# Sinkhorn by matmul, re-paced loads and crossbar transposes, and o a unit later, in a fused attention and FFN kernel on one core

## Chip, cores and metric

One core of a Trainium2 chip. The time is device microseconds of that core; spans (first to last instruction of a profiled execution) are about 1.8 us shorter than times. A transfer is *issued* when an engine puts it into its queue and *lands* when its data has arrived; "landed after" counts from the issue. With one core a run is called slow when it is over 1.5% above the fastest run of the same kernel in its session, otherwise fast. Ratios are the mean of one kernel's fast runs over the mean of the other's fast runs of the same rounds on the same chip, so they are not quite the ratios of the medians that are quoted beside them.

## The reference

```python
P = sort_net                                   # (4, 8, 8, 8)
for _ in range(5):                             # Sinkhorn
    P = exp(P - max(P, -1))
    P = P / (sum(P, -1) + 1e-9)
    P = P / (sum(P, -2) + 1e-9)
k_sorted = einsum('bhij,bhjcd->bhicd', P, k_blocks)      # 8 blocks of 96 rows, head dim 64
v_sorted = einsum('bhij,bhjcd->bhicd', P, v_blocks)
attn = softmax(q_blocks @ k_sorted.T / 8)                # inside each block
x = (attn @ v_sorted), heads side by side                # 3072 x 512
out = ((x @ w_a) * (x @ w_b)) @ w_out                    # d_ff 1536
```

q, k, v are 4 x 8 x 768 x 64, all in float32.

## The kernel before, cut

The work is done in 16 pairs of heads, g = 0 to 15, four to a batch (HP = 4). A pair goes through four steps. *mix*: k and v are mixed by P. *scores*: q times k and the exponential. *o*: times v, and normalized into xp. *xT*: xp transposed into the FFN's operand. Batch 0 is done in two halves with transposes on the matrix engine (PE). Batches 1 to 3 use crossbar transposes, DMA_TRANSPOSE, issued by SyncE (SP): q into qTf, mixed v into vs, xp into xT. GpSimd (POOL) issues all loads, which convert to bf16. The attention of batch b+1 is cut into "units" that are threaded between the FFN steps of batch b.

```python
for it in range(5):                       # Sinkhorn: 32 partitions (one a head), 64 elements each
    nc.scalar.activation(out=p_nat, in_=p_nat, func=AF.Exp)
    nc.vector.reduce_sum(out=rsum, in_=p_nat, axis=AX.X)
    nc.vector.reciprocal(out=rsum, in_=rsum)
    nc.vector.tensor_mul(...)             # rows
    nc.vector.reduce_sum(out=csum, in_=p_nat.transpose([0, 2, 1]), axis=AX.X)
    nc.vector.reciprocal(out=csum, in_=csum)
    nc.vector.tensor_mul(...)             # columns; then replicate, transpose by matmul, spread
...
def c_(g):                                # mix
    if g == HP:
        stage_q(g)                        # q transpose by crossbar, SP
    if g + 1 < B * HP:
        stage_q(g + 1)
    if g + 2 < B * HP:
        pair_q(g + 2)                     # GpSimd copy of q, ahead of its transpose
    if g + HP < B * HP:
        load_pair((g + HP) // HP, g % HP) # k, v, q of the pair one batch on
    stage_mix(g, "k", ("act",))
    stage_mix(g, "v", ("dve", "act"))     # ends with the v transpose by crossbar
def o_(g):
    stage_o(g)
    to_xT(g)                              # xp transpose by crossbar
for n in range(HP + 1):
    if n < HP: us.append(c_(g0 + n))
    if n > 0:  us.append(o_(g0 + n - 1))
    if n < HP: us.append(stage_scores(g0 + n))
```

`us.append(x(...))` stands for a closure. FFN steps are `ffn_ab` (eight matmuls of 384 columns, 1.3 us) and `ffn_out`, a "po step" (twelve of 512 columns, 2.6 us). The units are spread evenly over the number of steps, so that all are done two steps before a batch's end at the latest.

The softmax here doesn't subtract the row's maximum and nothing guards it: scores larger than these inputs give would overflow.

## Time and profile before

| | |
|---|---|
| median of the first 3 runs | 256.21 us (253.7 to 257.01) |
| profiled span | 252.7 us |
| PE busy | 234.4 us, 93% |
| PE waits for vs (v's crossbar transpose) | 5.4 us in two waits |

First, from the page of the kernel before, the span in 40 slices of 6.3 us. Digits are tenths; PEclk is the granted PE clock, and DMA the mean busy share of the 16 DMA engines.

```profile
PE   0999899969958999999999999999999999999993
PEclk9999999999997999999999999999999999999999
DMA  6999999999999998992332343332244210000122
```

PE is full but for its start, slice 9 and slices 12 and 13 (counted from 1), where it waits; in slice 13 the clock falls once. The DMA queue is full until about 115 us. The view of waits of PE names the two dips (us in total, times, the longest):

```profile
PE o_ps L241 <- DMA vs<-vT: 5.4, 2, 3.3
```

In PE's timeline (start, duration, line, tile, count) the later of them, and the end of batch 0, look so:

```profile
76.44 1.04 PE L241 MATMUL o_ps<-vs,eT 96*128 96x65 bf16 x16 [3.33 <-DMA vs<-vT]
77.29 4.02 PE L351 MATMUL po<-w_out_sb,hT 128*128 128x512 bf16 x12
...
84.29 0.66 PE L241 MATMUL o_ps<-vs,eT 96*128 96x65 bf16 x16
84.79 7.93 PE L351 MATMUL po<-w_out_sb,hT 128*128 128x512 bf16 x35
92.56 0.97 PE L323 MATMUL pf<-xT,w_a_sb 128*128 128x384 bf16 x4
```

After 3.33 us of waiting the sixteen o matmuls take 1.04 instead of 0.66 us and twelve po matmuls 4.02 instead of 2.76 (x11 and x35 stand for 12 and 36: some matmul records are missing from a trace): the wait is paid again in slow clock. Then o of the last pair at 84.29 us, three po steps, and batch 1's first FFN matmuls, which need its xT. SP's timeline of the same time:

```profile
69.06 5.00 SPq L262 DMA_TRANSPOSE qTf<-qc  x1
74.16 4.56 SPq L283 DMA_TRANSPOSE vs<-vT  x1
...
86.53 1.30 SPq L309 DMA_TRANSPOSE xT<-xp  x1
88.36 6.29 SPq L358 DMA_DIRECT2D out_dram<-o_sb  x6
94.75 1.27 SPq L262 DMA_TRANSPOSE qTf<-qc  x1
```

The view of the tile xT, narrowed to the transpose issued at 86.53 us, has its landing:

```profile
L309 SPq DMA_TRANSPOSE xT<-xp x1: 1301/1301/1301, 86.5 to 86.5; - x1
...
DMA to landing us min/median/max: 6.6/6.6/6.6
```

So the last xT landed at 93.1 us. PE's first three matmuls of batch 1 need pairs 0 to 2 only; the fourth needs the last pair.

At the start, two of the exponentials in ScalarE's timeline give a Sinkhorn round, 1.76 us; PE's timeline gives the first mix, a 512-column filler (a matmul whose result nobody uses, there to keep PE busy), and the first FFN matmul:

```profile
4.12 0.26 ACT L374 ACTIVATE p_nat<-p_nat 32x64 f32<-32x64 f32 x1 [1.50 <-DVE p_nat L387]
5.88 0.26 ACT L374 ACTIVATE p_nat<-p_nat 32x64 f32<-32x64 f32 x1 [1.50 <-DVE p_nat L387]
```

```profile
12.20 0.38 PE L191 MATMUL mixh<-s_all,k 128*64 128x64 bf16 x12
...
14.12 0.39 PE L166 MATMUL mixh<-warm 128*128 128x512 bf16 x1
...
20.59 0.66 PE L323 MATMUL pf<-xT,w_a_sb 128*128 128x384 bf16 x3
```

### The profile page before, as it was taken

To read this page: it belongs to the slowest core of one execution; us is meant where nothing else is said; L and a number is where in the kernel's file an instruction comes from. 1 tells how busy PE (TensorE), PEld (TensorE's weight loads), DVE (VectorE), ACT (ScalarE), POOL (GpSimd) and SP (SyncE) were. 2 spreads that over 40 slices of the span, in tenths; PEclk is the share of its full clock that TensorE was granted. 3 is DMA by queue.
4 is the path that set the end of the run, shared out by engine and by line. 5 is a ranking of instruction groups with operands and counts; after the bars stand their busy time and mean duration, and the time that the engine had idled before them with its cause. 6 is when DMAs were issued, how large, how long until landed. Compare 5 with 4: busy or idle time off the path is not lost.

```text
span 252.7 us, 5448 instructions
## 1 busy us (share of the span) xinstructions
PE 234.4 (93%) x2219; PEld 135.6 (54%) x2229; DVE 108.2 (43%) x259; ACT 102.4 (41%) x202; POOL 61.4 (24%) x83
## 2 busy tenths in 40 slices
PE   0999899969958999999999999999999999999993
PEld 0475566536624455666654456666654466665441
DVE  6775456535613313555453133645533144444111
ACT  3385555556520217463740137465440033333010
POOL 8974678554715305300100000000000000000000
PEclk9999999999997999999999999999999999999999
DMA  6999999999999998992332343332244210000122
GB/s 88 197 199 196 197 200 201 190 169 184 146 129 199 239 204 160 160 116 45 72 65 83 115 118 73 67 74 40 42 35 125 113 44 0 0 0 4 52 114 83
DMA packets 56441, 28.67 MB, mean 113 GB/s; under 512 B 33376, under 2 KB 53344, under 8 KB 56416
## 3 DMA queue, kind: packets, MB, share of 16 engines
q0 software_dynamic: 20944, 14.16, 40.6%
q1 hardware_dynamic: 35472, 14.17, 28.9%
q8 instruction: 17, 0.28, 0.4%
q14 instruction: 8, 0.07, 0.1%
HBM read 28.32 MB, written 6.29 MB: 137 GB/s over the span
## 4 chain that ended last, share of the span: by engine, by line
PE 83%; DMA 9%; DVE 5%; ACT 1%; issue 1%; DVEq 0%
PE pf L323 46%; PE po L351 24%; DMA vs<-vT 8%; PE o_ps L241 3%; PE mix L272 3%; PE sc L293 2%; PE mixh L191 2%; PE vs_ps L218 1%; PE sc L206 1%; PE xt_ps L232 1%; DMA p_nat<-in_sort_net_dram 1%; DVE hT L344 1%; DVE xph L247 1%; DVE csum L384 1%; ACT p_nat L374 1%
## 5 line engine op out<-in xcount | busy, mean ns | idle before, releaser
L344 DVE TENSOR_TENSOR hT<-a_sb,pf 128x384 bf16<-128x384 bf16 x95 | 52.6, 554 | 74.0 <-PE pf L323 45.5
L323 PE MATMUL pf<-xT,w_a_sb 128*128 128x384 bf16 x380 | 78.1, 327 | 0.0
L323 PE MATMUL pf<-xT,w_b_sb 128*128 128x384 bf16 x380 | 77.5, 326 | 0.0
L343 ACT CAST a_sb<-pf 128x384 bf16<-128x384 f32 x95 | 45.5, 479 | 65.9 <-PE pf L323 49.4
L351 PE MATMUL po<-w_out_sb,hT 128*128 128x512 bf16 x279 | 64.5, 385 | 0.5
L323 PEld LDWEIGHTS <-w_b_sb 128*128 128x128 bf16 x384 | 37.5, 98 | 25.1 <-issue 0.6
L323 PEld LDWEIGHTS <-w_a_sb 128*128 128x128 bf16 x384 | 34.6, 98 | 22.1
L351 PEld LDWEIGHTS <-hT 128*128 128x128 bf16 x288 | 28.0, 99 | 33.3 <-issue 1.6
L162 DVE COPY o_sb<-po 128x512 f32<-128x512 f32 x12 | 8.3, 692 | 47.8 <-PE po L351 31.3
L160 ACT COPY o_sb<-po 128x512 f32<-128x512 f32 x12 | 7.0, 586 | 43.0 <-PE po L351 23.1
L298 ACT ACTIVATE eT<-sc 96x768 bf16<-96x768 f32 x24 | 18.1, 802 | 12.4 <-PE sc L293 12.4
L256 POOL COPY qc<-q 128x768 bf16<-128x768 bf16 x12 | 9.9, 826 | 53.1 <-DMA qTf<-qc 34.0
L241 PE MATMUL o_ps<-vs,eT 96*128 96x65 bf16 x256 | 11.6, 196 | 6.1 <-DMA vs<-vT 5.4
L247 DVE TENSOR_TENSOR xp<-o_ps,rec 96x512 bf16<-96x512 f32 x24 | 15.5, 680 | 0.3
L241 PEld LDWEIGHTS <-eT 96*128 96x128 bf16 x256 | 10.5, 99 | 8.9 <-issue 6.3
L160 ACT CAST kT<-mix 128x384 bf16<-128x384 f32 x24 | 10.3, 482 | 6.2 <-PE mix L272 6.2
L94 POOL DMA_DIRECT2D v<-in_v_dram x16 | 11.5, 718 | 1.8 <-DMA w_b_sb<-in_moe_w_b_dram 0.8
L94 POOL DMA_DIRECT2D k<-in_k_dram x16 | 11.5, 719 | 1.2 <-DMA w_a_sb<-in_moe_w_a_dram 0.6
L245 DVE RECIPROCAL rec<-o_ps 96x8 f32<-96x8 f32 x32 | 5.2, 185 | 12.1 <-PE o_ps L241 12.0
L94 POOL DMA_DIRECT2D q<-in_q_dram x12 | 8.6, 719 | 1.3 <-DMA w_a_sb<-in_moe_w_a_dram 0.7
L175 PE MATMUL q_ps<-ident,q_first 64*64 64x64 bf16 x96 | 3.0, 217 | 6.2 <-DMA q_first<-in_q_dram 6.2
L210 ACT ACTIVATE eT<-sc 96x768 bf16<-96x768 f32 x8 | 6.5, 808 | 2.5 <-PE sc L206 2.5
(69 smaller groups left out, 138.4 us busy)
## 6 DMA issues: line engine op xcount, KB each, us to landing
out_dram<-o_sb SPq DMA_DIRECT2D x18, 256.0 KB, 2.0
k<-in_k_dram POOLq DMA_DIRECT2D x16, 192.0 KB, 6.4
v<-in_v_dram POOLq DMA_DIRECT2D x16, 192.0 KB, 6.8
q<-in_q_dram POOLq DMA_DIRECT2D x12, 192.0 KB, 9.1
w_a_sb<-in_moe_w_a_dram POOLq DMA_DIRECT2D x6, 256.0 KB, 10.8
w_b_sb<-in_moe_w_b_dram POOLq DMA_DIRECT2D x6, 256.0 KB, 10.7
w_out_sb<-in_moe_w_out_dram POOLq DMA_DIRECT2D x3, 512.0 KB, 10.9
out_dram<-o_sb SPq DMA_DIRECT2D x12, 128.0 KB, 5.1
```

The lines of the kernel that those rows point to most:

```text
L94: nc.gpsimd.dma_start(out=to, in_=_ap(t, base, [[W, P], [S * D, 2], [1, W]]))
L160: nc.scalar.copy(out=out, in_=in_)
L162: nc.vector.tensor_copy(out=out, in_=in_)
L241: nc.tensor.matmul(o_ps[:, e, i * (D + 1):(i + 1) * (D + 1)], lhsT=eT[:, hf, e, i * BLK:i * BLK + P], rhs=vs[0:BLK, i0 + i, V0 - 1 + e * ( ...
L247: nc.vector.tensor_tensor(out=_ap(xp, i0 * 2 * D, [[nxp * 2 * D, BLK], [D, 2], [2 * D, NBH], [1, D]]), in0=_ap(o_ps, 1, [[1024, BLK], [511 ...
L256: nc.gpsimd.tensor_copy(out=qc.rearrange("p c e d -> p e c d"), in_=loaded[g][2].rearrange("p e (c d) -> p e c d", c=NCH))
L272: nc.tensor.matmul(mix[e * D:(e + 1) * D, c // 3, c % 3 * P:(c % 3 + 1) * P], lhsT=src2[:, e, c * D:(c + 1) * D], rhs=s_all[:, 2 * g + e], ...
L298: nc.scalar.activation(out=eT[:, hf, :, 0:HB], in_=sc[0:BLK, :, 0:HB], func=AF.Exp, scale=float(scale))
L323: nc.tensor.matmul(pf[:, 0:HW], lhsT=w_sb[:, kc, m * P:(m + 1) * P], rhs=x_cols(b, kc, t), start=(kc == 0), stop=(kc == KA - 1))
L343: nc.scalar.copy(out=a_sb, in_=pf[:, 0:HW])
L344: nc.vector.tensor_mul(out=hT[:, m, t * HW:(t + 1) * HW], in0=a_sb, in1=ab[1][:, 0:HW])
L351: nc.tensor.matmul(po, lhsT=hT[:, m, c * P:(c + 1) * P], rhs=w_out_sb[:, m, :], start=(m == 0), stop=(m == KO - 1))
```

## The change

Its intent: a shorter Sinkhorn, by spreading it over 128 partitions, and no waits for vs, by keeping loads away from the transposes and giving v's transpose more time. Cut to its core:

```diff
 # Sinkhorn: partition = (head, column), 16 heads at a time, 8 elements each
+def sink_sum(g, it, ps):            # row sums by an fp32 matmul with a 128x128 block matrix
+    lhs, rhs = (sk[g, "rows"], is_block) if it == 0 else (heads, sk[g, "e"])
+    nc.tensor.matmul(ps, lhsT=lhs..., rhs=rhs, start=True, stop=True)
+def sink_vec(g, it, ps):            # reciprocal, multiply, reduce, reciprocal
+    ...
-    keep_busy(heat[:, 0], 8)        # filler matmuls before the first mix
+    # 2 fillers in rounds 1 and 2, 1 before the first mix
 # heads 0-15 at the start; heads 16-31 as six "turns" in FFN steps of batch 0's second stage,
 # the last of which lets GpSimd spread their P
 ...
 # q of batch 1: all its loads first, then all four copies and transposes
-for hp in range(2): load_pair(1, hp)
+for hp in range(HP): load_pair(1, hp)
 ...
-pair_q(HP); pair_q(HP + 1); for hp in range(2, HP): load_pair(1, hp)
+for g in range(HP, 2 * HP): pair_q(g); stage_q(g)
 def c_(g):
-    stage_q(g), stage_q(g + 1), pair_q(g + 2), load_pair(next batch)
     stage_mix(g, "k", ...); stage_mix(g, "v", ...)
 def o_(g):
     stage_o(g)
     to_xT(g)
+    if 2 * HP <= g + 2 < B * HP:
+        pair_q(g + 2); stage_q(g + 2)
+    if g + HP < B * HP:
+        nc.gpsimd.tensor_copy(out=gate, in_=st[g, "xp"][...one element])   # the "gate"
+        load_pair((g + HP) // HP, g % HP)
 # order of units: c_(g), scores(g), o_(g-1) instead of c_(g), o_(g-1), scores(g)
 # spacing: a po step counts as two ab steps (paced), two po steps left at the end
```

The spacing has a consequence: batch 0 now has two po steps after its last o instead of three, and batches 1 and 2 have three instead of four. Small things left out of the cut: the order of two loads at the start, the order of two units of batch 0's second half, and four buffers instead of three for q.

## The prediction

> **What bounds it now.** The matrix engine. The page has PE busy 234.4 of 252.7 us; the chain of waits that ended last is 83% PE. From 90 to 240 us the table of stretches shows PE busy in full; gains can come only from before:
>
> 1. Start: PE's timeline has the first mix at 12.20 us. Until then the chain is Sinkhorn on 32 partitions: each round is one exponential and six VectorE operations of 0.19 to 0.27 us, 1.76 us a round, then p_fin, p_rep, pc_ps, s_all, 1.29 us.
> 2. Two waits of the o matmuls for the crossbar transpose of v (vs): 2.12 us at 57 us and 3.33 us at 76 us (waits of PE, 5.4 us). After the second the clock fell: o takes 1.04 instead of 0.50 us and twelve po matmuls 3.83 instead of about 2.6. Together about 7.4 us. Alone a transpose lands in 3.0 us, beside the loads of batch 2 in 8 to 13, and SyncE's queue is in order: the v transpose of 74.16 us stood behind a q transpose that took 5.0 us to issue.
>
> **What changes.**
> - Sinkhorn, half of the heads: a round becomes an exponential, one small fp32 matmul and four VectorE operations on 8 elements a partition. The Trainium skill, "FP8 and Floating Point Precision", section TensorE Precision Notes, gives true fp32 four passes; no run here shows it yet. From pc_ps (four bf16 pairs, 0.36 us from operand ready to reader started) I estimate 0.45 us for the matmul. With 0.75 for VectorE and 0.30 for the exponential a round is about 1.5 us: 0.25 saved, four times. The tail loses a step (0.4 us). Against it: masks and memsets before round one, and a load in 32-byte pieces, 0.4 us. Net 0.8 us earlier.
> - The other half moves into batch 0's second stage: five fp32 matmuls and one more, about 1.8 us of PE, in PE's program order, each behind a VectorE and ACT round trip of about 2 us where a step gives 1.3 to 2.1. Estimate: 1.8 us of work, 1 us of stalls.
> - Loads of batch 2 wait for xp, q transposes of batch 1 go early, and o comes a unit later: v's transpose gets about 9 us instead of 4 to 5, on quieter queues. Both waits go, and the clock drop with them: 7.4 us less about 0.5.
> - New danger: batch 0's last o now leaves two po steps (5.2 us) instead of three before batch 1 needs its xT, and the late loads fall beside that transpose (6.6 us in this trace at 80 to 87 us). I charge 0.8 us at about 90 us.
>
> Sum: -0.8 -6.9 +2.8 +0.8 = -4.1 us for the profiled run. The profiled run took 254.5; the median, 256.2, probably holds larger transpose waits, which go too: about -6.
>
> **Predicted: 250.2 us**, range 247.3 to 253.3; faster by over 2% 0.63, within 2% 0.35, slower 0.02.
>
> **Right if:** waits of PE for vs below 1 us; no clock slice under 0.9 after the start; first mix at 11 to 11.8 us; rounds of 1.4 to 1.6 us; chain_b matmuls of group 1 with PE waits for ACT around 45 to 58 us; 90 to 240 us unchanged in length.
>
> **Wrong if:** the fp32 matmul takes well over 0.5 us (no gain at the start, more stall in stage 2); PE waits for xT near 88 us by 2 us or more, with a clock drop; the loads, now later, miss their mixes; or the turns hide entirely and the run lands below 248.

## The result, and the profile after

The result was correct and slower: 270.87 us median of four runs (270.58 to 279.17), against 256.61 us for before with one more run; the ratio of fast runs is 1.059, 95% interval 1.048 to 1.071. It is outside the predicted range and on the other side of before.

The same views after. The slices:

```profile
PE   3699899999999809999899958999999999999993
PEclk9999999999999977999999997999999999999999
DMA  6999999981599993018888895113141620000132
```

The waits of PE; vs is gone from the list, xT is at its top:

```profile
PE pf L382 <- DMA xT<-xp: 12.0, 2, 7.7
...
PE sc L352 <- DMA qTf<-qc: 0.9, 1, 0.9
```

The end of batch 0 in PE's timeline, then SP's and GpSimd's around it:

```profile
86.81 0.66 PE L300 MATMUL o_ps<-vs,eT 96*128 96x65 bf16 x16
87.52 5.12 PE L410 MATMUL po<-w_out_sb,hT 128*128 128x512 bf16 x23
92.49 0.65 PE L382 MATMUL pf<-xT,w_a_sb 128*128 128x384 bf16 x3
100.84 0.48 PE L382 MATMUL pf<-xT,w_a_sb 128*128 128x384 bf16 x1 [7.71 <-DMA xT<-xp]
```

```profile
85.96 1.21 SPq L368 DMA_TRANSPOSE xT<-xp  x1
87.27 1.24 SPq L321 DMA_TRANSPOSE qTf<-qc  x1
88.61 2.54 SPq L417 DMA_DIRECT2D out_dram<-o_sb  x2
91.24 1.53 SPq L368 DMA_TRANSPOSE xT<-xp  x1
92.86 3.19 SPq L321 DMA_TRANSPOSE qTf<-qc  x1
```

```profile
86.58 0.72 POOL L109 DMA_DIRECT2D k<-in_k_dram  x1 [0.34 <-issue]
...
90.38 0.72 POOL L109 DMA_DIRECT2D k<-in_k_dram  x1
```

The view of the tile xT, for the transpose issued at 91.24 us:

```profile
L368 SPq DMA_TRANSPOSE xT<-xp x1: 1527/1527/1527, 91.2 to 91.2; - x1
...
DMA to landing us min/median/max: 9.6/9.6/9.6
```

The last o starts at 86.81 us; its transpose is issued 4.4 us later (2.2 before), behind a q transpose and two stores in SP's queue; it lands 9.6 us after that (6.6 before), beside the loads that the gate released at 86.58 and 90.38 us; and one po step of cover is missing. That is 2.2 + 3.0 + about 2.6 us, the wait of 7.71 us. Afterwards nine FFN matmuls and a mix of k and v run on a slow clock, 1.8 us more. The end of batch 1 repeats it with a wait of 4.26 us.

The start, in ScalarE's and PE's timelines:

```profile
6.78 0.30 ACT L189 ACTIVATE e<-rc,c 128x8 f32<-128x8 f32 x1 [1.58 <-PE heat L180]
8.74 0.30 ACT L189 ACTIVATE e<-rc,c 128x8 f32<-128x8 f32 x1 [1.66 <-DVE c L216]
```

```profile
7.14 0.59 PE L205 MATMUL chain_a<-e,heads 128*128 128x8 f32 x2 [0.42 <-ACT e L189]
...
14.19 0.53 PE L250 MATMUL mixh<-s_all,k 128*64 128x64 bf16 x12 [0.47 <-DVE vs L151]
...
16.73 0.61 PE L180 MATMUL mixh<-warm 128*128 128x512 bf16 x1
...
25.46 0.67 PE L382 MATMUL pf<-xT,w_a_sb 128*128 128x384 bf16 x3
```

A round is 1.96 us, longer than before. The first mix comes 2.0 us later and the first FFN matmul 4.9 us later: the other 2.9 us lie in the attention between them, most of which runs on a slow clock; the same filler takes 0.61 instead of 0.39 us.

Where the 16.4 us of span went, by starts read from PE's timelines (us per stage; the last stage is to the end of the span). The other three columns are runs described below; the last is of a slow run, so it is not compared in time.

| stage | before | after | old start | gate only | gate, order, q (slow run) |
|---|---|---|---|---|---|
| to the first FFN matmul | 20.6 | 25.5 | 21.1 | 21.3 | 21.6 |
| to the first mix of batch 1 | 26.8 | 27.5 | 27.5 | 26.8 | 26.8 |
| to the first po step | 23.0 | 21.6 | 25.5 | 24.4 | 28.2 |
| to batch 1's first FFN matmul | 22.2 | 18.0 | 18.0 | 17.1 | 17.1 |
| to batch 2's | 54.7 | 65.1 | 65.0 | 55.0 | 69.2 |
| to batch 3's | 54.5 | 60.5 | 60.4 | 54.5 | 54.5 |
| to the end | 51.0 | 51.0 | 50.9 | 51.0 | 51.0 |

The forecast gain is there, 5.6 us in the third and fourth rows. It is lost twice over: 5.6 us in the first two rows, and 16.4 us in the rows of batches 1 and 2, which begin at the ends of batches 0 and 1: 12.0 us of waits for xT, one wait of 0.9 us for qTf, and nearly all the rest slow clock after the waits.

### The profile page after: what moved, and what is told of

The parts are those of the page before. It is cut to its first block, busy times and chain, and to the rows that moved or that the text cites. A ratio compares the mean times of both kernels' runs of the same rounds, so it can differ in the third digit from the quotient of the medians.

```text
span 269.1 us, 5501 instructions
## 1 busy us (share of the span) xinstructions
PE 241.0 (90%) x2226; PEld 141.2 (52%) x2238; DVE 111.3 (41%) x277; ACT 104.0 (39%) x207; POOL 62.1 (23%) x90
## 4 chain that ended last, share of the span: by engine, by line
PE 79%; DMA 10%; DVE 5%; ACT 2%; issue 1%; SPq 1%; DVEq 0%; ACTq 0%
PE pf L382 43%; PE po L410 20%; DMA xT<-xp 7%; PE mix L331 4%; PE o_ps L300 3%; DMA qTf<-qc 2%; PE sc L352 2%; PE mixh L250 2%; PE chain_a L205 1%; DVE hT L403 1%; PE vs_ps L277 1%; PE sc L265 1%; DMA p_nat<-in_sort_net_dram 1%; PE xt_ps L291 1%; SPq L417 1%
## 5 line engine op out<-in xcount | busy, mean ns | idle before, releaser
L382 PE MATMUL pf<-xT,w_a_sb 128*128 128x384 bf16 x380 | 79.1, 329 | 12.0 <-DMA xT<-xp 12.0
L382 PE MATMUL pf<-xT,w_b_sb 128*128 128x384 bf16 x380 | 78.7, 330 | 0.0
L410 PE MATMUL po<-w_out_sb,hT 128*128 128x512 bf16 x277 | 63.2, 379 | 0.7 <-issue 0.2
L410 PEld LDWEIGHTS <-hT 128*128 128x128 bf16 x288 | 27.3, 98 | 31.4
L357 ACT ACTIVATE eT<-sc 96x768 bf16<-96x768 f32 x24 | 18.2, 803 | 6.7 <-PE sc L352 6.7
L552 POOL COPY gate<-xp 1x1 bf16<-1x1 bf16 x8 | 1.4, 180 | 54.4 <-DVE xp L306 54.4
L315 POOL COPY qc<-q 128x768 bf16<-128x768 bf16 x12 | 9.9, 836 | 11.7 <-DMA q<-in_q_dram 11.7
L300 PEld LDWEIGHTS <-eT 96*128 96x128 bf16 x256 | 10.6, 99 | 3.2 <-ACT eT L269 0.7
L300 PE MATMUL o_ps<-vs,eT 96*128 96x65 bf16 x256 | 11.6, 196 | 0.6 <-ACT eT L269 0.6
L166 POOL TENSOR_TENSOR s_all<-mask,p_col 128x1024 bf16<-128x1024 bf16 (+1 forms) x4 | 6.7, 1696 | 20.2 <-DVE p_col L587 20.1
L176 DVE CAST vT<-mix 128x384 bf16<-128x384 f32 x12 | 6.7, 558 | 4.5 <-PE mix L331 4.5
```

The source lines that it names most:

```text
L176: nc.vector.tensor_copy(out=out, in_=in_)
L300: nc.tensor.matmul(o_ps[:, e, i * (D + 1):(i + 1) * (D + 1)], lhsT=eT[:, hf, e, i * BLK:i * BLK + P], rhs=vs[0:BLK, i0 + i, V0 - 1 + e * ( ...
L315: nc.gpsimd.tensor_copy(out=qc.rearrange("p c e d -> p e c d"), in_=loaded[g][2].rearrange("p e (c d) -> p e c d", c=NCH))
L357: nc.scalar.activation(out=eT[:, hf, :, 0:HB], in_=sc[0:BLK, :, 0:HB], func=AF.Exp, scale=float(scale))
L382: nc.tensor.matmul(pf[:, 0:HW], lhsT=w_sb[:, kc, m * P:(m + 1) * P], rhs=x_cols(b, kc, t), start=(kc == 0), stop=(kc == KA - 1))
L410: nc.tensor.matmul(po, lhsT=hT[:, m, c * P:(c + 1) * P], rhs=w_out_sb[:, m, :], start=(m == 0), stop=(m == KO - 1))
```

## The experiments

Eighteen more kernels were run; all gave correct results. "Before" medians varied from 255.6 to 258.0 us from session to session, so ratios are given. Medians are over all runs, slow ones too; ratios are of fast runs alone; spans are of the profiled run.

| run | this, median us | ratio to before (95%) | span | PE waits in the profile, us |
|---|---|---|---|---|
| after | 270.9 | 1.059 (1.048 to 1.071) | 269.1 | xT 12.0, qTf 0.9 |
| old_start | 270.9 | 1.052 (1.042 to 1.062) | 268.4 | xT 11.7, qTf 5.4 |
| old_pace | 259.1 | 1.006 (0.999 to 1.013) | 257.0 | xT 1.7, vs 0.6 |
| no_gate | 266.4 | 1.035 (1.028 to 1.042) | 264.4 | xT 7.6 |
| spare4 | 267.5 | 1.038 (1.029 to 1.047) | 265.0 | qTf 4.2, xT 1.7, o_sb 1.9 |
| pe_last_x | 265.0 | 1.039 (1.035 to 1.043) | 262.5 | qTf 6.7, o_sb 1.7 |
| delay | 261.8 | 1.028 (1.023 to 1.032) | 260.0 | vs 5.9 |
| o_later | 256.1 | 0.996 (0.989 to 1.003) | 251.5 | vs 3.1 |
| gate_only | 251.0 | 0.984 (0.977 to 0.991) | 250.0 | vs 1.9, xT 0.3 |
| gate_paced | 254.7 | 0.994 (0.985 to 1.003) | 253.2 | xT 5.0, vs 0.5 |
| gate_o_later | 252.4 | 0.987 (0.979 to 0.994) | 251.1 | xT 2.8 |
| gate_newq | 254.8 | 0.994 (0.984 to 1.005) | 254.1 | qTf 4.8, xT 1.0 |
| gate_newsink | 254.3 | 0.985 (0.974 to 0.996) | 252.8 | xT 0.8 |
| gate_paced_o | 259.4 | 1.004 (0.984 to 1.024) | 259.4, slow run | xT 8.5 |
| gate_paced_q | 261.3 | 1.010 (0.986 to 1.035) | 258.7 | qTf 5.0, xT 3.3 |
| gate_o_q | 269.1 | none, one fast run | 268.3, slow run | qTf 9.4, xT 6.0 |
| fix_pe | 253.4 | 0.990 (0.979 to 1.002) | 248.7 | vs 0.9, o_sb 0.8 |
| after_oldq | 265.0 | 1.036 (1.024 to 1.047) | 263.5 | vs 3.1, xT 2.4 |
| warm_sink | 255.3 | none, one fast run | 249.3 | xT 0.4 |

### The two halves apart

**old_start** is the changed kernel with before's Sinkhorn.

```diff
-    sink_exp / sink_sum / sink_vec / turns, heads 0-15 at the start
+    the Sinkhorn loop of before, all heads, keep_busy(heat[:, 0], 8)
```

> The changed kernel with the Sinkhorn of before (32 partitions, all heads at the start, its eight filler matmuls), everything else of the change kept. Theory A, two separate causes: the new Sinkhorn costs the 4.9 us by which the first pf matmul came later (25.5 against 20.6 us) and about 2 us in its turns, the new pacing costs the rest by waits for xT at the ends of batches 0 and 1. Then: first pf at 20.5 to 21 us, PE waits for xT still 8 us or more in sum, time 262 to 266 us. Rival B: the xT waits come from the Sinkhorn too, because its second half held GpSimd, and so the loads behind it, until 70.6 us. Then: xT waits below 2 us in sum and time 248 to 252 us.

Measured: first FFN matmul at 21.1 us, just above A's range, xT waits of 11.7 us, as A said, but 270.9 us: nearly as slow as the whole change. B is out: with no second half of Sinkhorn the xT waits stay. A's sum is out too, because the 4.4 us won at the start were lost again in the third row of the table, at a new wait in PE's timeline:

```profile
55.05 0.52 PE L294 MATMUL sc<-qTf,kT 64*128 64x96 bf16 x16 [4.23 <-DMA qTf<-qc]
```

The q transposes of batch 1 now wait for all its loads. They were issued from 43.4 us on and landed at 55 us, whatever PE does; a later start hides this, an earlier one shows it.

**old_pace** is before with the new Sinkhorn alone.

```diff
-    the Sinkhorn loop of before
+    sink_exp / sink_sum / sink_vec, heads 16-31 in turns; loads, q, units, spacing of before
```

> The kernel of before with the new Sinkhorn alone (both halves of it, the second in turns), and the loads, q transposes and units of before. Theory A: first pf at 25 to 26 us, PE waits for vs of 3 to 7 us as before, PE waits for xT below 1 us, time 261 to 265 us. Rival B: the xT waits of 8 us or more are there too and the time is 266 us or more.

Measured: first FFN matmul at 26.3 us, but only 0.6% slower, the wait for vs nearly gone (0.6 us), and a wait for xT of 1.7 us, a little above A's and far below B's. So the new pacing is what costs, and B is wrong here too. Why the later start cost so little was a new question. GpSimd's timeline suggests an answer: its spread of the second half's P stood in its queue until the turns were done, and the loads of batch 2's last two pairs (issued at 73.58 and 76.54 us) stood behind it.

```profile
69.09 3.77 POOL L166 TENSOR_TENSOR s_all<-mask,p_col 128x1024 bf16<-128x1024 bf16 x2 [10.19 <-DVE p_col L580]
```

That would be a gate by accident. It is a reading, not shown, and gate_newsink below speaks against it as the whole answer. A rival reading, that until 76 us the DMA queue sets the time and so any late start is absorbed, was tested with **delay**:

```diff
-            keep_busy(heat[:, 0], 8)
+            keep_busy(heat[:, 0], 28)
```

> The kernel of before with 28 instead of 8 filler matmuls ahead of the first mix: PE starts its real work about 4.5 us later, nothing else is changed. Theory C: until about 76 us the time is set by the DMA queue (loads and the transposes beside them), so a later start is taken out of the waits for vs. Then first pf at 25 us, waits for vs fall from 5.4 to below 2 us, and the time rises by less than 2 us, to 256 to 258.5 us. Rival D: PE's start is on the critical path, as the prediction had it. Then the time rises by the whole delay, to 260.5 to 261.5 us.

Measured: first FFN matmul at 26.05 us, waits for vs still 5.9 us, and 2.8% slower, about 7 us. Theory C is wrong; loads are issued from inside the units, so they move with PE. D is right in kind; the loss is even larger than the delay of 5.5 us, the rest being slow clock after the waits (0.76 to 0.90 of full in three stretches of 5 us).

### Inside the changed kernel

**no_gate** and **spare4** each undo one thing.

```diff
-                nc.gpsimd.tensor_copy(out=gate, in_=st[g, "xp"][0:1, NB - 1, 1, D - 1:D])
```

> The changed kernel without the one-element GpSimd copy that makes each load of the next batch wait for xp; GpSimd then issues the loads as soon as it reaches them. Theory A1: the last xT transpose of a batch is late because the gate puts the last loads beside it. Then its landing falls from 9.6 to 4 to 6 us, the PE waits for xT fall from 12.0 to 4 us or less, some wait for vs may come back, and the time is 259 to 264 us. Rival A2: the last o simply comes too near the batch's end, and SyncE's queue holds it up; then landing or issue stay late, the waits stay above 8 us and the time is 268 us or more.

Measured: 266.4 us, between the two theories. The xT waits fell to 7.6 us, but the last two xT transposes still landed 9.2 and 9.6 us after issue: without the gate GpSimd went on issuing loads, a pair every 2 to 7 us, from 72 to 111 us, across the end of the batch. The gate alone is not the cause.

```diff
-        paced(ab, po, units_full(b + 1) if b + 1 < B else [], 2)
+        paced(ab, po, units_full(b + 1) if b + 1 < B else [], 4)
```

> The changed kernel with all units done four po steps before the end of a batch instead of two; the gate stays, so the loads move forward with the last o. Rival A2 (too little cover): xT waits fall from 12.0 to below 3 us with landing still 8 to 10 us, time 258 to 262 us. Theory A1 (the loads beside it) alone: the transposes still land late, 8 to 10 us after issue, and the cover of about 10 us hides most of it, so A1 also predicts a fall here; what tells them apart is the landing time in the run without the gate. If neither is right the waits stay above 8 us.

Measured: xT waits 1.7 us with landings of 10.6 and 10.7 us, as A2 said, but 267.5 us instead of 258 to 262. The wait moved: scores of batch 2 waited 4.2 us for qTf, and an FFN matmul 1.9 us for the copy of an output tile (o_sb).

**pe_last_x** takes the last xp of a batch off the crossbar: eight PE transposes and two copies, in a unit of its own.

```diff
             stage_o(g)
-            to_xT(g)
+            if g % HP < HP - 1:
+                to_xT(g)
+        us.append(lambda: x_(g0 + HP - 1))      # PE transposes of the last pair
```

> The changed kernel, but the last pair of each batch brings its xp to xT by eight PE transposes and two copies, as the first batch does, instead of by the crossbar; all loads, the gate and the other transposes stay. If the late crossbar transpose of the last xp is what costs at the ends of batches 0 and 1, the PE waits for xT fall from 12.0 us to below 1.5, the clock stays at 1.0 around 100 and 160 us, and the time falls from 270.9 to 255 to 260 us. If the ends of the batches wait for something else (q or v transposes of the next batch, or the loads themselves), a wait of 5 us or more turns up at another tile near 100 us and the time stays above 264 us.

Measured: no wait for xT at all, and yet 265.0 us. Scores waited 6.7 us for qTf instead, in three places. So neither "the xT wait" nor "the cover" is the cause by itself; take one late transpose out of the way and the next one shows.

### From before upwards

Two single pieces on before. **o_later** is only the order of units:

```diff
-                if n > 0:
-                    us.append(lambda g=g0 + n - 1: o_(g))
                 if n < HP:
                     us.append(lambda g=g0 + n: stage_scores(g))
+                if n > 0:
+                    us.append(lambda g=g0 + n - 1: o_(g))
```

> The kernel of before with only the order of units changed: scores before the o of the pair before (o a unit later). v's transpose gets one unit more, 2 to 3.5 us, so the waits for vs fall from 5.4 to below 2 us. Against it, scores come a unit earlier and their q transposes do not: by the trace of before the q transpose of pair 7 landed at 81.2 us and its scores started at 81.25 us, so a wait of scores for qTf of 2 to 4 us should appear. If that trade is right the time stays within 2 us of before; if the q transposes move forward too, it falls to 249 to 252 us.

Measured: same time, waits for vs 3.1 us, and the foreseen wait for qTf did not come. **gate_only** is only the loads:

```diff
 def c_(g):
-    if g + HP < B * HP:
-        load_pair((g + HP) // HP, g % HP)
 def o_(g):
     stage_o(g)
     to_xT(g)
+    if g + HP < B * HP:
+        nc.gpsimd.tensor_copy(out=gate, in_=st[g, "xp"][0:1, NB - 1, 1, D - 1:D])
+        load_pair((g + HP) // HP, g % HP)
```

> The kernel of before with only the loads moved: each load of the next batch is issued after the o of its pair and waits for xp, as in the change. If the gate is what puts loads beside the last xT transpose, PE waits for xT appear at the ends of batches 0 and 1 (before leaves three po steps of cover, not two, so 1 to 5 us in sum) while the waits for vs fall below 1.5 us; time 252 to 258 us. If the gate is innocent, no xT wait appears and the time is 248 to 251 us.

Measured: 0.984 of before, an interval clear of 1, though not clear of 2%. The wait for xT is 0.3 us. **The gate is the good part of the change**; with before's three po steps of cover it does no harm. It is faster than both kernels. One wait for vs is left, and PE's timeline shows what even a short one costs:

```profile
57.65 0.65 PE L242 MATMUL o_ps<-vs,eT 96*128 96x65 bf16 x16 [1.95 <-DMA vs<-vT]
58.14 1.04 PE L324 MATMUL pf<-xT,w_a_sb 128*128 128x384 bf16 x4
58.97 1.49 PE L324 MATMUL pf<-xT,w_b_sb 128*128 128x384 bf16 x4
```

Eight FFN matmuls take 2.25 us from start to next start (58.14 to 60.39), where before has 1.40 at the same place; the following scores and four more matmuls lose another 0.7.

### One part more

Each of the next four adds one part of the change to gate_only: the spacing (the `paced` loop), the order of units, the late q transposes (`pair_q`, `stage_q` moved as in the change), and the new Sinkhorn. Their edits are the parts of the diff above.

> The run with only the gate (251.0 us) plus only the new spacing of units, which counts a po step as two ab steps and leaves two po steps after the last o of batch 0 instead of three (three instead of four for batches 1 and 2). Theory E1, too little cover under the gate: PE waits for xT rise from 0.3 us to 4 us or more, with a clock drop, and the time is 255 to 262 us. If the spacing is innocent, xT waits stay below 1 us and the time is 249 to 252.5 us.

Measured: the xT wait of 5.0 us came with its slow clock; 254.7 us, at the edge of the expectation, same as before.

> The run with only the gate plus only the order of units (scores before the o of the pair before). The one wait for vs left with the gate, 1.9 us, should go, and no wait for xT come, as the last unit of a batch is the last o either way: 247.5 to 250.5 us. If the gate, which follows o, now brings the loads later and nearer the batch's end, an xT wait of 1 us or more appears and the time is 251 to 254 us.

Measured: the wait for vs went, and an xT wait of 2.8 us came: the last two o are now neighbours, so the loads behind the last but one fall beside the last xT transpose, which lands after 9.4 us instead of 6.9. No gain, no loss.

> The run with only the gate plus only the new q transposes: those of batch 1 all together after all its loads, those of later batches after the o of two pairs before instead of one stage before their scores. Theory E2: scores wait for qTf of batch 1 near 50 us by about 4 us, because the transposes start only when the last load of batch 1 and the w_out loads are issued, and the q transposes beside the last xT cost up to 2 us more of xT wait; time 254 to 260 us. If the q transposes are innocent, no wait for qTf over 1 us and 249 to 252 us.

Measured: scores wait 4.8 us for qTf at 55 us and FFN matmuls 1.0 us for xT, as E2 said; the slowest of these spans.

> The run with only the gate plus the new Sinkhorn. In the run with the new Sinkhorn alone, its second half held GpSimd until 69.1 us and so delayed the loads of batch 2, a gate by accident; with the gate in both, that gain is no longer in the difference. Theory F: the new Sinkhorn costs what it costs at the start (first pf 4.9 to 5.7 us later) and in its turns (1.5 to 3 us), together 6 to 8 us: 257 to 259.5 us. Rival: it is nearly free, as its 0.6% alone said: below 253.5 us.

Measured: ratio 0.985, as gate_only's. Theory F is wrong in size: the first FFN matmul came at 25.15 us, 3.8 us later than in gate_only, but the span only 2.8 us later. The later start again let the loads land, and the 1.95 us wait for vs was gone. With the gate in both kernels the new Sinkhorn is still nearly free, so the accidental gate can't be the main reason why it was so in old_pace.

So three parts of the pacing each cost 0.3 to 1% on top of the gate, by ratios from two chips whose intervals overlap. Added, their single spans give 250.0 + 3.2 + 1.1 + 4.1 = 258.4 us; together (old_start, with the small things named above) they gave 268.4. About ten microseconds belong to the combination, more than the spread of one kernel's fast runs (2 to 4 us), and pairs were run to find it.

> Gate, spacing and order together, old q transposes. Theory G (shared slack): each part takes a bite of one reserve, the time from the last o of a batch to the first need of its xT; a part alone is nearly free, parts together cost in full. Then the wait for xT at the end of batch 0 is 6 us or more (5.0 and 2.8 alone, 0.3 with the gate alone) and a wait of 1 to 4 us appears at the end of batch 1, where no part alone had one: 257 to 262 us. Rival H (the parts add, and the q transposes are the rest): the spans add to 250.0 + 3.2 + 1.1, so 255 to 256.5 us, no wait at the end of batch 1.

Measured: xT waits 8.5 us, among them the foreseen new one at the end of batch 1, 2.23 us; 256 to 261 us. The times alone do not decide between G and H. The profiled run is slow, and its start fell on a slow clock (first FFN matmul at 24.9 us), so its xT waits, which look like G's, settle nothing.

> Gate, spacing and new q transposes, old order of units. Theory G: the wait for qTf near 52 us stays at 4 to 5 us, the wait for xT at the end of batch 0 is 5 to 8 us, a wait of up to 2 us at the end of batch 1; 260 to 264 us. Rival H: the spans add to 250.0 + 3.2 + 4.1, so 258 to 260 us.

Measured: 256.7 to 263.8 us; the profiled run is fast, 260.5 us, where the ranges of G and H meet; its span of 258.7 us is 1.4 above H's sum; the xT wait, 3.3 us, is smaller than G said.

> Gate, order and new q transposes, old spacing. Theory G: the wait for qTf near 52 us stays at 4 to 5 us, the wait for xT at the end of batch 0 is 3 to 6 us, none at the end of batch 1 (four po steps of cover); 257 to 260 us. Rival H: 250.0 + 1.1 + 4.1, so 256 to 258 us; or, if the last missing 10 us sit in order and q together, 262 us or more.

Measured: 263.2 us in the only fast run and 269 to 270 in the others, against 253 to 260 for before in the same rounds. The last branch of H was hit, by one fast run: the missing time sits in order and q together. The view of waits of PE (of a slow run, so its sizes are not to be relied on; the fast run too is 6 us above the additive 257):

```profile
PE sc L294 <- DMA qTf<-qc: 9.4, 3, 4.6
...
PE pf L324 <- DMA xT<-xp: 6.0, 1, 6.0
```

In the old arrangement a q transpose goes into SP's queue one pair ahead of its scores, before the mix. In the new, it goes in behind the o of two pairs before; with o a unit later and scores a unit earlier, only one mix is left between. And at a batch's end the order puts xT, q, xT, q closely after each other into SP's queue, with the loads that the gate releases: in old_start, a fast run, at 85.54, 86.85, 89.47 and 92.15 us. There the last xT landed 10.7 us after its issue, 13.8 us after its o started (11.6 and 14.8 us in the slow run of gate_o_q).

The three pairs can also be read as old_start less one part (on another chip, and without the small things named above). With all three parts the ratio is 1.052; without the late q transposes (gate_paced_o) 1.004, without the order (gate_paced_q) 1.010, with intervals clear of old_start's. Without the spacing (gate_o_q) the one fast run stays over 3% above before's fast runs of its session. So most of old_start's loss needs order and late q transposes both.

### Back in the changed kernel

**after_oldq** puts only the q transposes of the changed kernel back.

```diff
 def c_(g):
+    if g == HP: stage_q(g)
+    if g + 1 < B * HP: stage_q(g + 1)
+    if g + 2 < B * HP: pair_q(g + 2)
 def o_(g):
-    if 2 * HP <= g + 2 < B * HP: pair_q(g + 2); stage_q(g + 2)
 # and batch 1's loads and q transposes in two pairs, as in before
```

> The changed kernel with only its q transposes put back (batch 1's in two pairs of loads, every later one at the mix of the pair before its scores). Theory I: in the whole change the late q transposes together with the later o are the main cost, as in the pair of the two alone. Then the waits for qTf are below 1 us, the wait for xT at the end of batch 0 falls from 7.7 to 3 to 6 us and the time from 270.9 to 258 to 263 us. Rival: cover and gate are enough for the loss; then xT waits stay above 10 us in sum and the time is above 266 us.

Measured: no wait for qTf, xT waits 2.4 instead of 12.0 us, and 265.0 us, 5.9 us better by medians but 2 us short of the expectation (ratio 1.036 instead of 1.059). The xT wait fell by more than the time because another transpose was late:

```profile
90.47 1.04 PE L300 MATMUL o_ps<-vs,eT 96*128 96x65 bf16 x16 [3.12 <-DMA vs<-vT]
```

So late q transposes account for some two fifths of the loss here, and not for all of it. Nor do they stand out: undoing the gate (1.035), giving more cover (1.038) or taking the last xT off the crossbar (1.039) takes back as much within the noise, and each time a wait for some late transpose or output copy was left. No single part is the cause. Undoing only the order, or only the spacing, in the full change was not tried.

### The start

**warm_sink** is gate_newsink with 21 fillers instead of 5 during the Sinkhorn (the expectation says 22; what it calls passes are the two records of each fp32 matmul in the trace).

```diff
+    keep_busy(heat[:, 0], 5)
     for it in range(5):
-        if it == 1 or it == 2: keep_busy(heat[:, 0], 2)
+        keep_busy(heat[:, 0], (2, 3, 4, 2, 3)[it])
-    keep_busy(heat[:, 0], 1)
+    keep_busy(heat[:, 0], 2)
```

> Gate and new Sinkhorn (254.3 us, span 252.8), with 22 filler matmuls of 512 columns instead of 5 during the Sinkhorn, so that PE is at full clock in it. Theory J: the new Sinkhorn's rounds are long because its fp32 matmul runs on a slow clock (0.59 us for its two passes at the start, 0.39 us in the second stage), and the attention of batch 0 after it too. Then rounds fall from 1.96 to 1.70 to 1.80 us, the first mix comes at 12.9 to 13.4 us, the first pf at 21 to 22 us instead of 25.15, and the time falls by 2 to 4 us, to 250.5 to 252.5. If the fillers stand in the matmul's way, rounds stay at 1.9 us or more and the first pf above 24 us.

Measured: half right. The first FFN matmul came at 21.9 us instead of 25.15, and the profiled span was 249.3 instead of 252.8 us. But rounds stayed at 1.86 to 1.95 us, the first mix came at 13.58 us, and of the four times one was 251.1 and three 255.2 to 255.7, so the gain in time is not shown. The fp32 matmul does shrink at full clock:

```profile
8.96 0.36 PE L205 MATMUL chain_a<-e,heads 128*128 128x8 f32 x2
```

The rounds did not follow: the first three sums still took 0.59 to 0.60 us, the clock being up only from about 9 us on, and in the fourth round a copy of q on ScalarE stood before the last exponential. But from the first mix to the first FFN matmul it took 8.36 us, as in before (8.39), where gate_newsink took 11.27: with the fillers that stretch is at full clock again. pe_last_x gives more evidence, by chance. It has the start of the changed kernel to the letter, and there the clock came up early (PE's timeline):

```profile
16.54 0.39 PE L180 MATMUL mixh<-warm 128*128 128x512 bf16 x1
...
23.01 0.66 PE L382 MATMUL pf<-xT,w_a_sb 128*128 128x384 bf16 x3
```

Filler 0.39 instead of 0.61 us; first mix at 14.00 against 14.19 us, first FFN matmul at 23.01 against 25.46. So of the 4.9 us 2.0 lie before the first mix and 2.3 are slow clock after it; the last 0.6 us was not followed up.

### A version faster than both

**fix_pe** joins the gate, the order, and the last xT by PE, with everything else of before.

> Gate and order of the change, with the q transposes, spacing and Sinkhorn of before, and the last pair of each batch brought to xT by PE transposes. No PE wait for vs or xT over 0.5 us should be left between 45 and 200 us, for about 1 us of PE transposes: 247.5 to 250.5 us, faster than before by 2 to 3%. If waits move to qTf or to the copies, it stays at 251 us or above, the time with the gate alone.

Measured: 250.5 to 254.8 us; by fast runs 0.990 of before, interval 0.979 to 1.002. Its profiled span, 248.7 us, is the shortest of all, with no wait over 0.8 us after 50 us, but its time is not shown to be below before's. Three versions have an interval wholly below 1: gate_only (0.984), gate_newsink (0.985) and gate_o_later (0.987); they all have the gate, and gate_only is the simplest.

## Why the prediction was wrong

- **"Both waits go": right.** The vs waits fell from 5.4 us to none, their slow clock with them: 5.6 us won in the third and fourth stages, against 4.1 forecast for them (6.9 less 2.8 for the turns, which lie there too).
- **"New danger ... I charge 0.8 us at about 90 us": this is the step that failed.** The mechanism was named, its size was off twentyfold: 16.4 us in the two stages after batch ends (12.0 of it waits for xT), not 0.8 at one. Three terms make the 7.71 us at the end of batch 0. Issue: 4.4 us after o, not the 2.2 of before, with a q transpose and two stores now ahead in SP's queue. Landing: 9.6 us, not 6.6, beside two sets of loads that the gate ties to the last two o (without the gate other loads ran there, and it landed after 9.2 and 9.6 us all the same). Cover: one po step less, which the prediction did see. Each was in the diff. With its own 6.6 us of landing, the 2.2 us to issue that before's trace shows, and a cover of two po steps and three FFN matmuls, a wait of about 2.7 us should have been charged, and before's landing at 93.1 us for a need at 93.05 showed that every lost microsecond would be paid in full. The end of batch 1 (three po steps, a wait of 4.26 us) was not considered.
- **The slow clock after a wait stands in the sum as a gain, not as a cost** (the list of what would be wrong names it). It added 1.8 us to the wait of 7.7 us. The Trainium skill, "TensorE: Matmul & The Clock Gate", section "What's actually happening", gives the mechanism, a clock gate that follows PE's activity; the trace agrees (0.52 of full clock from 100 to 105 us).
- **"Net 0.8 us earlier": wrong in sign.** First mix 2.0 us later: 0.4 up to the first exponential (as forecast), 0.9 in four rounds, 0.7 in the tail. A round's terms: exponential to matmul 0.36 us (forecast 0.30), matmul 0.63 (0.45), VectorE 0.97 (0.75). VectorE operations on 8 elements take 0.16 to 0.21 us where those on 64 took 0.19 to 0.25: they hardly shrink with their size. The tail from the last exponential to the first mix grew from 2.81 to 3.49 us.
- **Not foreseen at the start: 2.9 us more from the first mix to the first FFN matmul**, 2.3 of it slow clock (pe_last_x); with fillers ahead of the first mix again (warm_sink) that stretch was as short as in before. Yet in the full change the whole new Sinkhorn cost only 0.7 us of span (269.1 against old_start's 268.4): with the old one, scores waited for q transposes instead.
- **The turns: about right.** PE waits for ScalarE of 0.8 us and about 1.8 us of fp32 matmuls in the second stage (forecast 1.0 and 1.8).
- **"90 to 240 us unchanged in length": wrong**, for the same reason as the second point: the batch ends lie in it.

What is shown: the loss is in the pacing, not the Sinkhorn (old_start, old_pace); the gate is a gain by itself (gate_only); order and late q transposes cost far more together than apart (old_start against gate_paced_o and gate_paced_q, and gate_o_q's one fast run); in the changed kernel undoing any one of four things takes back about two fifths of the loss at most. What is only argued: that it is the order within SP's queue and the loads beside it, rather than something else in the DMA engines, which makes landings grow from 3 us to between 9 and 12. What stays open: how the loss divides among the parts of the full change, and the time gained by a warm Sinkhorn.

## What to carry to other kernels

Ahead of moving a transfer, write down for each consumer three times from the trace: producer to issue (with what now stands ahead in that in-order queue), issue to landing under the traffic that will be there, and the work that covers them; where before has no reserve, every part of a change that touches one of the three is paid in full and parts add up worse than their single tests say. Gates that follow a producer also gather traffic just behind it, so look at what else follows the same producer. Try the parts of a bundle one by one on the old kernel: here the best part alone beat both the old kernel and the bundle.

## What the Trainium skill lacked or had wrong

- "DMA: Bandwidth & Descriptors", section "Rules for kernel authors", says that "A transpose next to ordinary DMAs needs nothing". For correctness these runs agree. For time they do not: one SBUF to SBUF crossbar transpose landed in 2.7 to 3.0 us on a quiet queue and in up to 12.9 us beside the loads; the page has a bandwidth for transposes, but no time to landing, alone or beside loads.
- "TensorE: Matmul & The Clock Gate", section "What's actually happening", has the clock fall after at least one idle window of about 3.4 us. Here it fell after a wait of only 1.95 us (gate_only: granted clock 0.86 and 0.80 in the 5 us stretches from 55 us on) and cost 1.5 us; a wait of 2.12 us in before, at 57 us, left it at 1.00. So the length of a wait alone does not tell whether the clock falls.
- "TensorE: Matmul & The Clock Gate", section "Seeing it yourself", warns that clock events in a trace can be unreliable. What it lacks is this case of it: the profile's granted clock reads 1.00 from 10 to 20 us in the changed kernel, where a 512-column filler takes 0.61 us instead of 0.39.
- "FP8 and Floating Point Precision", section "TensorE Precision Notes", gives true fp32 four passes. The trace has two records for each fp32 matmul of 128x128 by 8, together 0.59 us on the slow clock and 0.36 to 0.39 us on the full one; the page has no duration for so small a product. Whether a record holds two passes is not shown.
